# Reordering the passes of a two-matrix feed-forward: three, two, three pairs of F blocks in place of three, three, two

## The chip, the cores and the metric

The kernel runs on one core of a Trainium2 chip. The metric is the device time of one execution in microseconds; three runs of the kernel before gave 1417.96, 1418.64 and 1419.7 us, so the median is 1418.64 us.

## What is computed

Three layers follow each other on 4608 tokens of 512 features:

```python
ret = (scale * q @ k.T) * decay        # retention, 8 batches x 8 heads x 576 positions x 64
x = (ret @ v), rearranged to (4608, 512)
x = mixture of 8 experts, top 1:  gate * (relu(x @ w1[e]) @ w2[e])     # 512 -> 1024 -> 512
h = relu(x @ w_in)                     # 512 -> 2048
out = (h * h) @ w_out                  # 2048 -> 512
```

All inputs are float32 (w_in and w_out are handed over as 64-bit words). The change concerns only the last two lines, the feed-forward with F = 2048.

## The kernel before, in words

`phase0` computes the retention and the routing, `phase12` the experts and meanwhile the preparation of the feed-forward weights, `phase3` (lines 1100 to 1332) the feed-forward. Phase 3 takes the second half of the time, from about 650 us on.

**Tiles.** Phase 3 works on 9 tiles of 512 tokens in the order in which the experts wrote them. Every product is done in a seven-product scheme on 2 x 2 blocks: a tile of x is turned into 7 combinations (`XT`, 7 buffers of 512 KB, one for each combination and none spare), a weight block into 7 combinations, and each operand is split into a high and a low part, so that one product is three matmuls. F is cut in 8 *pairs* of 128-blocks (`NFP = 8`), each pair with its own combined weights for w_in (`WT[0]`) and w_out (`WT[1]`), two 896 KB arrays (high and low) for each.

**Passes.** The weights of all 8 pairs don't fit in SBUF. There are slots for three pairs, so phase 3 goes over the tokens three times. `PASSES` (line 40) says which pairs each pass works on; `T3` (line 1312) lists the steps: pass 0 goes over tiles 0 to 8, pass 1 from 8 down to 0, pass 2 over 0 to 8 again, so that the tile at each turn is the same and its x combinations stay in place. A step has 2 x 7 x (number of pairs) groups of six matmuls of 128x256: `one` (first product, accumulated in PSUM, then squared relu by DVE and ACT into `z`, then split into `h`) and `two` (second product, added by DVE into the output tile `OE`). That is 252 matmuls in a step with three pairs and 168 with two.

**Partial outputs.** There are two output tiles in SBUF, `oe` and `yr` (`OE`, line 1113), used in turn. In passes 0 and 1 a finished tile of partial sums goes to DRAM (`pd`, line 1295, two halves of 512 KB on SP's queue). In passes 1 and 2 `begin(n)` (line 1298) loads the partial sums of tile n back (two halves of 512 KB on SP's queue); a half can be loaded only when the tile that used the buffer before, two steps earlier, has left it. In the last pass (`ends`, line 1260) the finished tile is instead scattered to `out` by four indirect DMAs of 128 rows each, issued by POOL (line 1290); each of them waits for the one before it.

**Loads.** `xprep` (line 1164) computes the x combinations in pass 0 and stores them to `xc`; in passes 1 and 2 it loads the 7 of the next tile (7 x 512 KB). `loadw` (line 1158) loads the weights of a pass into the slots 0, 1 (and 2): those of w_in are planned behind `one` of the last step of the pass before, those of w_out behind its `two`; a slot can be loaded as soon as its last reader is done. All plain DMAs of phase 3 go through SP's queue, which issues them in a fixed order and stands still while the first of them waits.

**Order.** The class `Plan` (line 1033) collects all operations of phase 3 with what they read and write, and orders them by a list scheduler with assumed durations: it looks at the next 400 operations that are left, takes what can start earliest and among these what is due earliest. The order of each engine's program, SP's and POOL's queues included, follows from that. A matrix operation knows nothing of the pass it belongs to, except that pass 0 copies where passes 1 and 2 add, and that the last pass scatters where the others store.

Of the kernel before, what the change touches and what calls it, by code (L numbers as in the profile page):

```python
# [36 lines left out]
CV = 512  # L37
NFP = FF // 256
NCV = 2 * NFP
PASSES = ((0, 1, 2), (3, 4, 5), (6, 7))  # L40
F64MIN = 1.125 * 2.0 ** -15


# [47 lines left out]
def kernel(ctx, tc, qT, kT, kN, vN, modT, w_gate, mbias, w1, w2, w_in, w_out,  # L91
# [929 lines left out]
    def wload2(m, j, pool_, load=True):  # L1021
        for x in range(2):
            held["w", m, j, x] = pool_.tile([P, 7, 256], F32R, tag="w", name=f"w{m}{j}{x}")
            if load:
                sp.dma_start(held["w", m, j, x].bitcast(F32).rearrange("p m c -> p (m c)"), wc[m, PASSES[0][j], x])

# [73 lines left out]
    def phase3():  # L1100
        with ExitStack() as c2:
# [39 lines left out]
            def dma(o, i, kb, r, w, early=False):  # L1141
                plan.add(m_(kb), lambda e: (pool if early else e).dma_start(o, i), r, w, 2.0)
# [15 lines left out]
            def loadw(p, m, j0=0):  # L1158
                for j, fp in list(enumerate(PASSES[p]))[j0:]:
                    for x in range(2):  # L1160
                        dma(WT[m][j][x].bitcast(F32).rearrange("p m c -> p (m c)"), wc[m, fp, x], 917,
                            [], [("w", m, j, x)])
# [40 lines left out]
            def one(n, q, x):  # L1203
                p, t = T3[n]
                if x == 1:
# [12 lines left out]
                         [("w", 0, q, 0), ("w", 0, q, 1), ("x", mx, 0), ("x", mx, 1)], [kp])  # L1218
                last = q == len(PASSES[p]) - 1
                if x == 1:  # L1220
# [37 lines left out]
            def two(n, x):  # L1258
                p, t = T3[n]
                ends = p == len(PASSES) - 1  # L1260
                c = "X" if x in (1, 6, 7, 4) else ("Z" if x == 2 else "Y")
                ps, kr = BR[c], ("R", c)
                for q in range(len(PASSES[p])):
                    u = HS_[n, q]
# [33 lines left out]
            def begin(n):  # L1298
                p, t = T3[n]
                if p and T3[n - 1][1] != t:  # L1300
                    v = VO[n]
                    oe = OE[v]
                    for j0 in (0, 2):
# [3 lines left out]
                            512, [("pd", t, j0)], kk)  # L1307
                if p == len(PASSES) - 1:
                    dma(ixs[n % 2], sd[t * TS:t * TS + TS].rearrange("(j p) -> p j", p=P), 2, [],
# [64 lines left out]
```

## Time and profile before

| what | value |
|---|---|
| median of three runs | 1418.64 us |
| the profiled execution | 1417.05 us, its span 1415.2 us, mean granted clock 0.981 |
| PE busy | 1346.4 us (95%), 10640 matmuls |
| DVE busy | 1024.9 us (72%) |
| ACT busy | 624.1 us (44%) |
| POOL busy | 170.5 us (12%) |
| DMA | 332.43 MB, mean 235 GB/s |

PE's share is that of an engine that sets the pace nearly everywhere, so what matters are the few places where PE stands, and the stretch behind its last matmul. A row of waits says which engine, line and tile waited for what, in total, how often and the longest. A row of the timeline gives start, duration, engine, line, operation, the tile written and those read, how many, and in brackets the idle time of the engine before it and what ended that. SPq is the queue of SyncE, which only issues DMAs.

### The profile page before, as it was taken

The numbers are of one execution on the slowest core, as the hardware profiler recorded it, in microseconds if no ns is written. First come the engines' busy times: TensorE is split into PE (matmuls) and PEld (weight loads), VectorE is DVE, ScalarE is ACT, GpSimd is POOL, SyncE is SP. The second block draws the span as 40 slices with busy tenths as digits, with TensorE's granted clock in tenths as the row PEclk, the third lists the DMA queues.
The fourth block names the chain that finished last, engine by engine and source line by source line (L and its number), as shares of the span: only waits on it lengthen the run. The fifth ranks groups of instructions, "written<-read, shape, count | busy, mean of one in ns | idle before, by whom it ended". The sixth has DMA issues, their size and how long they took to land. (4 is left out here: it accounts for less than half of the span.)

```text
span 1415.2 us, 26973 instructions
## 1 busy us (share of the span) xinstructions
PE 1346.4 (95%) x10640; PEld 1236.5 (87%) x10640; DVE 1024.9 (72%) x2042; ACT 624.1 (44%) x1285; POOL 170.5 (12%) x166
## 2 busy tenths in 40 slices
PE   6999998999999999988999999999999999999985
PEld 5888776888788888878899999999999999999984
DVE  2787766878787788554788877867666777688764
ACT  1444344445445454344555555554334444334321
POOL 3222202100110010000311112000000000011112
PEclk9999999999999999998999999999999999999998
DMA  9988247988999897799544554477445565787672
GB/s 328 382 294 301 91 149 248 258 256 204 326 280 260 237 322 197 232 280 270 202 179 179 199 213 184 191 306 263 165 165 203 214 212 191 275 276 283 224 255 102
DMA packets 143782, 332.43 MB, mean 235 GB/s; under 512 B 20256, under 2 KB 54560, under 8 KB 143648
## 3 DMA queue, kind: packets, MB, share of 16 engines
q1 hardware_dynamic: 135520, 310.06, 65.3%
q0 software_dynamic: 5920, 19.40, 3.6%
q8 instruction: 85, 1.39, 0.4%
q10 hardware_dynamic: 2208, 1.17, 0.3%
q14 instruction: 49, 0.40, 0.1%
HBM read 222.57 MB, written 108.02 MB: 234 GB/s over the span
## 5 line engine op out<-in xcount | busy, mean ns | idle before, releaser
L1153 PE MATMUL bank<-w,h 128*128 128x256 f32 x1008 | 285.0, 283 | 8.9 <-DVE h L1254 8.8
L1151 PE MATMUL bank<-w,h 128*128 128x256 f32 x1008 | 284.1, 282 | 8.2 <-DVE oe L1129 7.3
L1152 PE MATMUL bank<-x,w 128*128 128x256 f32 x1008 | 285.4, 283 | 1.3 <-DVE x L1129 1.3
L1151 PE MATMUL bank<-x,w 128*128 128x256 f32 x1008 | 285.5, 283 | 0.9 <-DMA x<-xc 0.5
L1152 PE MATMUL bank<-w,h 128*128 128x256 f32 x1008 | 283.9, 282 | 1.8 <-DMA w<-wc 1.8
L1153 PE MATMUL bank<-x,w 128*128 128x256 f32 x1008 | 285.0, 283 | 0.0
L1126 ACT ACTIVATE z<-bank 128x256 f32<-128x256 f32 x288 | 109.3, 381 | 275.6 <-PE bank L1153 249.9
L1153 PEld LDWEIGHTS bank<-w,h 128*128 128x128 f32 x1008 | 190.9, 189 | 11.4 <-DVE h L1254 11.2
L1151 PEld LDWEIGHTS bank<-w,h 128*128 128x128 f32 x1008 | 191.2, 190 | 9.8 <-DVE oe L1129 7.9
L1152 PEld LDWEIGHTS bank<-x,w 128*128 128x128 f32 x1008 | 192.9, 191 | 1.9 <-DVE x L1129 1.9
L1151 PEld LDWEIGHTS bank<-x,w 128*128 128x128 f32 x1008 | 192.6, 191 | 1.4 <-ACT z L1126 0.6
L1153 PEld LDWEIGHTS bank<-x,w 128*128 128x128 f32 x1008 | 193.0, 191 | 0.0
L1152 PEld LDWEIGHTS bank<-w,h 128*128 128x128 f32 x1008 | 190.7, 189 | 2.1 <-DMA w<-wc 2.0
L1253 ACT ACTIVATE h<-z 128x512 fp32r<-128x512 f32 (+2 forms) x270 | 158.1, 599 | 68.0 <-DVE z L1129 46.7
L1254 DVE TENSOR_TENSOR h<-z,h 128x512 fp32r<-128x512 f32 (+2 forms) x270 | 172.4, 666 | 3.7 <-ACT h L1253 3.7
L1129 DVE TENSOR_TENSOR z<-z,bank 128x256 f32<-128x256 f32 x216 | 89.5, 417 | 58.9 <-PE bank L1153 53.4
L800 PE MATMUL bank<-hh,wy 128*128 128x512 f32 (+1 forms) x320 | 126.8, 396 | 4.0 <-ACT hh L816 4.0
L800 PE MATMUL bank<-xh,wx 128*128 128x512 f32 (+1 forms) x320 | 124.5, 389 | 3.8 <-PEq L917 3.8
L801 PE MATMUL bank<-xl,wx 128*128 128x512 f32 (+1 forms) x320 | 124.1, 388 | 1.1 <-DVE xl L756 1.1
L801 PE MATMUL bank<-hl,wy 128*128 128x512 f32 (+1 forms) x320 | 124.2, 388 | 0.7 <-DVE hl L817 0.7
L1129 DVE TENSOR_TENSOR z<-z 128x256 f32<-128x256 f32 x288 | 121.8, 451 | 3.1
L802 PE MATMUL bank<-xh,wx 128*128 128x512 f32 (+1 forms) x320 | 124.0, 387 | 0.0
(167 smaller groups left out, 2178.8 us busy)
## 6 DMA issues: line engine op xcount, KB each, us to landing
x<-xc SPq DMA_DIRECT2D x112, 512.0 KB
wr<-w SPq DMA_DIRECT2D x80, 512.0 KB
xc<-x SPq DMA_DIRECT2D x63, 512.0 KB
w<-wc SPq DMA_DIRECT2D x32, 896.0 KB
wc<-cwh SPq DMA_DIRECT2D x16, 896.0 KB
wc<-cwl SPq DMA_DIRECT2D x16, 896.0 KB
pd<-oe SPq DMA_DIRECT2D x24, 512.0 KB
xd<-xs SPq DMA_DIRECT2D x9, 1024.0 KB
```

Source lines behind the costliest of these rows:

```text
L800: pe.matmul(ps, lh, rh, start=first, stop=False)
L801: pe.matmul(ps, lh, rl, start=False, stop=False)
L802: pe.matmul(ps, ll, rh, start=False, stop=last)
L1126: plan.add(a_(c), lambda e: e.activation(o, i, f), r, w)
L1129: plan.add(engs or d_(c), lambda e: e.tensor_tensor(out=o, in0=a, in1=b, op=op), r, w)
L1151: e.matmul(ps[n], lh, rh, start=first and n == 0, stop=False, skip_group_check=True)
L1152: e.matmul(ps[n], lh, rl, start=False, stop=False, skip_group_check=True)
L1153: e.matmul(ps[n], ll, rh, start=False, stop=True, skip_group_check=True)
L1253: plan.add(a_(c), lambda e: e.activation(h[:, 0, a:b], z[:, a + 1:b + 1], AF.Copy), rs, ks[0])
L1254: plan.add(d_(c), lambda e: e.tensor_tensor(out=h[:, 1, a:b], in0=z[:, a + 1:b + 1], in1=h[:, 0, a:b].bitcast(F32), op=ALU.subtract), rs + ...
```

## The change

One line: the middle pass has two pairs and the last has three.

```diff
-PASSES = ((0, 1, 2), (3, 4, 5), (6, 7))
+PASSES = ((0, 1, 2), (3, 4), (5, 6, 7))
```

Everything else follows from `PASSES`: the number of pairs in `one` and `two` of each step, the weights that `loadw` loads at each turn (before: three pairs at the first turn and two at the second; after: two and three), and with them the order that `Plan` makes.

## Rows read from the trace of the kernel before

**Rows 1.** Waits of PE, 942 to 1400 us (passes 1 and 2): total, times, longest.
```profile
PE bank L1151 <- DVE oe L1129: 7.3, 3, 6.2
PE bank L1153 <- DVE h L1254: 1.0, 2, 0.6
PE bank L1151 <- DMA x<-xc: 0.5, 1, 0.5
```

**Rows 2.** Windows: length, busy us (instructions) by engine, clock, DMA share, GB/s.
```profile
core 0: us, PE busy (x) PEld busy (x) DVE busy (x) ACT busy (x) POOL busy (x), PEclk, DMA share, GB/s
971.50:1181.50 210.00, 210.00 (x1773) 210.00 (x1773) 151.92 (x322) 91.40 (x212) 0.00 (x0) 1.00 0.54 194
...
1240.00:1340.00 100.00, 100.00 (x847) 100.00 (x846) 82.15 (x177) 39.19 (x93) 18.07 (x17) 1.00 0.77 267
1340.00:1360.00 20.00, 13.84 (x104) 13.63 (x103) 9.91 (x21) 4.50 (x12) 4.47 (x4) 0.83 0.66 230
1385.00:1400.00 15.00, 12.78 (x95) 11.38 (x93) 12.08 (x26) 3.56 (x8) 4.05 (x4) 1.00 0.35 116
...
1211.00:1231.00 20.00, 19.49 (x162) 19.11 (x162) 14.96 (x32) 8.85 (x20) 0.00 (x0) 1.00 0.89 354
```

**Rows 3.** Timeline of PE and DVE around the one long stand in pass 2.
```profile
1330.63 0.69 DVE L1129 TENSOR_TENSOR yr<-yr,bank 128x512 f32<-128x512 f32 x1 [0.82 <-PE bank L1153]
...
1342.44 0.28 PE L1153 MATMUL bank<-w,h 128*128 128x256 f32 x1
1348.14 0.69 DVE L1129 TENSOR_TENSOR oe<-oe,bank 128x512 f32<-128x512 f32 x1 [6.46 <-DMA oe<-pd]
1348.88 0.58 PE L1151 MATMUL bank<-w,h 128*128 128x256 f32 x1 [6.17 <-DVE oe L1129]
```

**Rows 4.** Timeline of POOL in pass 2: scatters, first of the second to sixth tile.
```profile
1252.58 0.97 POOL L1290 DMA_INDIRECT out<-yr,ix  x1 [3.47 <-DVE z L1129]
...
1340.41 1.05 POOL L1290 DMA_INDIRECT out<-oe,ix  x1 [5.40 <-DMA out<-oe,ix]
1343.96 0.97 POOL L1290 DMA_INDIRECT out<-yr,ix  x1 [2.50 <-issue]
```

**Rows 5.** The tile out: time from a scatter's issue to its landing.
```profile
DMA to landing us min/median/max: 2.7/5.8/7.2
```

**Rows 6.** Timeline of SP's queue: loads of partial sums in pass 2.
```profile
1332.15 0.32 SPq L1142 DMA_DIRECT2D oe<-pd  x1
...
1343.34 0.32 SPq L1142 DMA_DIRECT2D oe<-pd  x1
```

**Rows 7.** Waits of SP's queue, 1200 to 1415 us (pass 2).
```profile
SPq L1142 <- DMA out<-oe,ix: 49.6, 7, 9.8
SPq L1142 <- DMA out<-yr,ix: 35.5, 6, 8.7
```

**Rows 8.** Timeline of POOL, DVE and PE at the end of the kernel.
```profile
1397.58 0.97 POOL L1290 DMA_INDIRECT out<-yr,ix  x1 [2.02 <-DMA out<-yr,ix]
...
1398.44 0.69 DVE L1129 TENSOR_TENSOR oe<-oe,bank 128x512 f32<-128x512 f32 x1 [0.47 <-PE bank L1153]
...
1399.54 0.28 PE L1153 MATMUL bank<-w,h 128*128 128x256 f32 x1
...
1399.86 0.69 DVE L1129 TENSOR_TENSOR oe<-oe,bank 128x512 f32<-128x512 f32 x1 [0.73 <-PE bank L1153]
...
1401.06 0.97 POOL L1290 DMA_INDIRECT out<-oe,ix  x1 [2.51 <-DVE oe L1129]
...
1410.54 0.97 POOL L1290 DMA_INDIRECT out<-oe,ix  x1 [2.02 <-DMA out<-oe,ix]
```

**Rows 9.** Timeline of SP's queue in pass 1: stores, and x loads.
```profile
970.37 2.43 SPq L1142 DMA_DIRECT2D pd<-oe  x2
974.12 1.56 SPq L1142 DMA_DIRECT2D oe<-pd  x2
978.23 7.49 SPq L1142 DMA_DIRECT2D x<-xc  x7
1000.98 2.43 SPq L1142 DMA_DIRECT2D pd<-yr  x2
```

**Rows 10.** Timeline of SP's queue at the second turn: weights of w_out.
```profile
1208.04 3.65 SPq L1142 DMA_DIRECT2D w<-wc  x4
```

## The prediction, made before the changed kernel was run

> **What bounds the kernel now.** First I read the waits of PE, because PE is busy for 95% of the span. In passes 1 and 2 they are three rows [rows 1]: PE stood for 7.3 us because of DVE's adds into `oe`, 6.2 us of it at once, 1.0 us for `h`, and 0.5 us for an x load. No row names weights, so both turns are covered today. Then the windows [rows 2]: in seven steps of pass 1 and in 100 us of pass 2 PE is busy without a gap at full clock, so a step costs what its matmuls cost. A matmul takes 210 / 1773 = 0.118 us there, so a three-pair step of 252 is 29.8 us (a store to the next store is 1000.98 - 970.37 = 30.6 us, [rows 9]) and a two-pair step of 168 is 19.9 us. Only the window from 1340 to 1360 us falls out: 104 matmuls, and a granted clock of 0.83.
>
> The timeline says why. PE's last matmul before the stand starts at 1342.44 us, the next at 1348.88 us, released by a DVE add, and that add by the landing of `oe<-pd` [rows 3]. This half of the partial sums was issued only at 1343.34 us, though the other half was issued at 1332.15 us [rows 6]; what held it is the fourth scatter of the tile that used `oe` before, issued at 1340.41 us [rows 4]. So the chain is scatter, load, add, PE. It is late because scatters are slower than the steps: from 1252.58 to 1343.96 us POOL issued 16 of them, 5.71 us each, 22.8 us for a tile of four [rows 4], against a step of 19.9 us. The queue of scatters falls back by some 2.9 us a step, more when waits add up: the output tile whose add is at 1330.63 us [rows 3] has its first scatter at 1343.96 us, 12.6 us after the add's end. SP's queue stood 85 us in pass 2 for landings of scatters (49.6 + 35.5, [rows 7]). Last I read the end: behind PE's last matmul (1399.82 us) there are 15.4 us of four scatters, each behind the other [rows 8].
>
> **The change part by part.** The matmuls, the DVE and ACT operations and the bytes stay what they are: pairs move from pass 1 to pass 2. What moves is which step has how much time.
>
> *The last pass gets 30 us steps.* Four scatters at 5.71 us are 22.8 us, so each tile's scatters end inside the next step, and no backlog builds up. A buffer is free some 23 us after its tile ends, plus the median landing of 5.8 us [rows 5] and the 4.8 us that the late load took (1343.34 to 1348.14), 34 us. When it is wanted: the tile before in `oe` ended, as an estimate, one step of 19.9 us before the add that ends at 1331.3 us [rows 3], so at 1311.4 us, and PE could go on without the next add into `oe` until 1342.7 us; that is 31 us or 1.57 steps, and 1.57 steps of 29.8 us are 47 us. The cover is 13 us. So the stand goes. Its price is the lost matmuls: 20 us of a full window hold 20 / 0.118 = 169, there were 104, so 65 x 0.118 = 7.7 us; 6.2 us of it is standing, and the rest is the lower clock behind it (granted 0.83 over that window, so a part of it at 1.2 GHz). Bounds: 0, if the stand comes back elsewhere, and 7.7 us. I take 7.7, since nothing near it in time is late next.
>
> The Trainium skill (DMA: Bandwidth & Descriptors, Anatomy of one DMA) gives a software-queue transfer as about 2.0 us plus its bytes at 436 GB/s; for 256 KB that is an estimate of 2.6 us. The trace has 2.7 us as the least and 5.8 us as the median [rows 5], so that figure fits a quiet queue only. By it four scatters would take 4 x (0.97 + 2.6) = 14.3 us, and the last pass would never have fallen behind, as in rival C.
>
> *The end.* In the last tile the first scatter is issued at 1401.06 us, though its adds ended at 1398.44 + 0.69 = 1399.13 us; POOL had issued the tile before only at 1397.58 us and came 2.51 us later, which is backlog again [rows 8]. With three pairs the last product behind that add is three groups of six (18 x 0.118 = 2.1 us) in place of two (1.4 us), so the add ends some 1.3 us before PE does, in place of 0.7. Without backlog the first scatter comes some 0.2 us after the add, 1.1 us before PE's end, where it is 1.24 us behind it now: 2.3 us less. The chain of four behind it (1401.06 to 1415.2, 14.1 us) stays. Bounds: 0, if a scatter is still in the way, and 2.5 us. I take 2.3.
>
> *PE's gaps in the last tile.* From 1385 us to PE's end, 14.8 us, there are 95 matmuls where 14.8 / 0.118 = 125 fit: 30 are missing, 3.5 us, with a few unrecorded ones among them [rows 2]. There is no next tile to work on while the last pair's z and h are made, and DVE is busy 12.08 of 15 us. With three pairs the second product has half as much again to do meanwhile, and the DVE load per matmul is lower (151.92 / 1773 = 86 ns in pass 1 against 82.15 / 847 = 97 ns in pass 2). Bounds: a loss of 0.5 us, if the chain of the last pair is as long and begins later, and a gain of 3.5. I take 1.5.
>
> *The middle pass gets 19.9 us steps.* Each has 7 x loads, two loads and two stores of partial sums, 11 x 0.524 MB = 5.8 MB, 290 GB/s. Pass 2 has the same bytes (the stores are scatters there) and moved 267 GB/s in its even part; right after the second turn it moved 354 GB/s [rows 2], so the demand fits. The buffer of the partial sums, which ruled pass 2, is free at once: from the first store's issue to the load that follows it are 3.75 us [rows 9], against the 23 us of scatters. The x loads stand behind the stores in SP's queue; there they begin 7.9 us after the first store (970.37 to 978.23). I expect this to be hidden, because in pass 2 SP was held up to 9.8 us at once and 85 us in all [rows 7], with the same 19.9 us steps, and x cost PE 0.5 us. Bounds: 0 and 2.9 us a step (rival A). I take 0.5 us in all.
>
> *The turns.* At the first turn four w_out arrays come in place of six; their 3.67 MB at 354 GB/s are 10.4 us, and they are wanted after one `one` of two pairs, 84 x 0.118 = 9.9 us, in part a little later. The second turn of before is this same turn, with its arrays issued at 1208.04 us [rows 10] and no wait of PE for w, but 0.5 us for x [rows 1]. At the second turn of after, slot 2 is free during the whole middle pass, so its four arrays can come early, and the rest has a three-pair step. I expect the 0.5 us for x to change places; bounds 0 and 3 us.
>
> **Sum**, against the profiled execution: -7.7 - 2.3 - 1.5 + 0.5 = -11.0, so 1417.05 - 11.0 = 1406.0 us. The runs' median stands 1.6 us above the profiled execution, which gives 1407.6 us for a median.
>
> **The rivals.**
> *A, slower: SP's queue starves the middle pass of x.* The two stores wait for the step's last adds, and seven x loads stand behind them. If the cover in a 19.9 us step is 5 us and not the 7.9 us from store to x load, each of 8 steps loses 2.9 us, 23 us in all; 1407.6 + 23 = 1430 us. It turns the sign from 11.5 / 8 = 1.4 us a step. For it: there is no spare x buffer, and the demand is 290 GB/s. Against it: the waits of pass 2 just named. By the Trainium skill (DMA: Bandwidth & Descriptors, Queues, rings and completion order) an engine drains one ring in order and shares between queue rows, so stores now stand ahead of x where scatters only shared; no run here shows that apart.
> *B: the weights are late at the turns.* Four arrays arrive in 10.4 us where 9.9 us are there, beside x loads. Two stands of some 3 us and, as after the stand of pass 2, 1.5 us of low clock each (7.7 - 6.2) make 9 us; 1416.5 us. Against it: the turn of before did the same without a wait.
> *C: the stand of pass 2 is no backlog.* Then it comes back in a last pass of any length, and only the end gains: 1407.6 + 7.7 = 1415 us. Against it: POOL's 5.71 us a scatter.
>
> **How the numbers follow.** Forecast 0.73 (own range 1404 to 1412), A 0.08, B 0.12, C 0.07. The forecast's lowest takes all upper bounds of gains, 7.7 + 2.5 + 3.5 = 13.7, so 1418.6 - 13.7 = 1405, and a us below it for run to run; the range goes up into B and C, to 1416. A change under 0.2% (2.8 us) can't be told from none. Faster: the forecast and half of B and of C, 0.82; same: their other halves, 0.1; slower: A, 0.08.
>
> **What would show it.** In the waits of PE no row of some 6 us for `oe`, and no window of passes 1 and 2 under 0.95 of the clock; scatters of a tile that begin within a us or so of its add, with idle POOL between tiles, and SP's waits for `out` far under 85 us; the last tile's first scatter before PE's last matmul. Wrong would be: a row of waits for x or w of over 2 us (A, B), a window of the middle pass with under 160 matmuls in 20 us (A), a stand for `oe` in the last pass (C).

## The result, and the profile after

The changed kernel took 1404.72 us (median of 4 runs, 1404.27 to 1407.67) beside 1418.3 us for the kernel before (4 runs, 1415.94 to 1419.7): 13.6 us less by the medians, a ratio of 0.989 with a 95% interval of 0.9852 to 0.9929. The direction and the mechanism were forecast; the size was forecast too small, 11.0 us. The median lies inside the range, but taken at the ratio, 0.989 x 1418.64 = 1403.0 us lies just under it, and in two further comparisons below the gain was 20 and 17 us by the medians.

PE's waits in passes 1 and 2 after the change (942 to 1400 us; engine, what it waited for, total, times, longest), which answer to [rows 1], and SP's waits for landings of scatters in the whole last pass (1120 to 1403 us), which answer to [rows 7]:

```profile
PE bank L1151 <- DVE oe L1129: 1.5, 1, 1.5
PE bank L1153 <- DVE h L1254: 1.4, 2, 0.7
PE bank L1151 <- ACT h L1253: 0.6, 1, 0.6
...
SPq L1142 <- DMA out<-oe,ix: 22.3, 4, 8.2
SPq L1142 <- DMA out<-yr,ix: 13.2, 3, 8.0
```

The stand of 6.2 us for `oe` is gone; the 1.5 us left is in the last tile. SP's queue stands 35.5 us for scatters in place of 85. Windows of the changed kernel, which answer to [rows 2] (the middle pass, the last pass, the 14.8 us before PE's end, the second turn; columns as there):

```profile
962.00:1100.00 138.00, 138.00 (x1164) 137.89 (x1164) 113.12 (x244) 57.77 (x127) 0.00 (x0) 1.00 0.87 316
...
1160.00:1380.00 220.00, 220.00 (x1855) 219.94 (x1855) 163.19 (x354) 96.12 (x210) 30.56 (x30) 1.00 0.52 183
...
1375.12:1389.92 14.80, 13.34 (x110) 12.90 (x108) 11.18 (x24) 3.40 (x7) 0.97 (x1) 1.00 0.01 2
...
1100.00:1120.00 20.00, 18.75 (x153) 18.22 (x152) 15.66 (x33) 7.32 (x16) 0.00 (x0) 1.00 0.74 289
```

In these windows the short pass moves 316 GB/s and PE doesn't stand once; the last pass is full too, at 183 GB/s. Scatters of the changed kernel, from the timeline of POOL, which answer to [rows 4] and [rows 8]:

```profile
1240.25 0.97 POOL L1290 DMA_INDIRECT out<-yr,ix  x1 [16.87 <-DVE yr L1129]
...
1270.14 0.97 POOL L1290 DMA_INDIRECT out<-oe,ix  x1 [11.99 <-DVE oe L1129]
...
1388.79 0.97 POOL L1290 DMA_INDIRECT out<-oe,ix  x1 [18.06 <-DVE oe L1129]
...
1398.27 0.97 POOL L1290 DMA_INDIRECT out<-oe,ix  x1 [2.02 <-DMA out<-oe,ix]
```

Between two tiles POOL is idle for 10.7 to 18.1 us: no tile's scatters reach the next tile's, and each tile's first scatter starts 0.28 us after the add that it waits for. The time from a scatter's issue to its landing, as [rows 5] has it:

```profile
DMA to landing us min/median/max: 2.7/3.0/4.3
```

This row and [rows 5] can't be set against each other. Each program has 36 scatters, and both profiles recorded the landing of only four of them; the profile of the changed kernel that recorded all 36 has a median of 4.4 us. POOL's timeline has every scatter, and it shows a smaller difference: from the first scatter of a tile to its fourth, over the first seven tiles, 11.3 to 18.7 us in three profiles of the changed kernel and 16.4 to 23.1 us in six of the kernel before. The scatters became somewhat faster; what ended the backlog is that each tile's four now have a step of 29.8 us.

**One measure for all profiles.** Up to the last step of pass 0 the programs of the two orders are the same, and their time there differs from execution to execution. So I take the store at the end of the eighth step of pass 0 as a mark (911.04 us in the first profile of before, 908.99 us after) and split what follows: from the mark to PE's end, and from there to the end of the span.

| profile | mark to PE's end | to the span's end | landing, median us (recorded, of 36) | us a scatter |
|---|---|---|---|---|
| before, first | 488.8 | 15.4 | 5.8 (4) | 5.71 |
| before, second | 490.0 | 14.7 | 4.7 (13) | 5.55 |
| before, third | 500.7 | 14.6 | 5.1 (36) | 6.13 |
| before, fourth | 495.5 | 15.2 | 4.8 (36) | 5.92 |
| before, fifth | 500.4 | 15.3 | 5.4 (36) | 6.26 |
| before, sixth | 500.4 | 14.9 | 4.9 (36) | 6.14 |
| after, three profiles | 480.9, 481.0, 481.7 | 13.0, 13.0, 13.0 | 3.0 (4), 4.1 (8), 4.4 (36) | |
| before, plain stores | 480.5 | 6.3 | 3.0 (4 stores) | |
| after, plain stores | 481.2 | 6.1 | 4.2 (8 stores) | |
| before, no x loads in the last pass | 478.9 | 13.7 | 2.8 (36) | |

The last column is the time from the first scatter of the second tile to the first of the sixth, divided by 16, as in [rows 4].

In the first pair of profiles the change brings 488.8 + 15.4 - 480.9 - 13.0 = 10.3 us behind the mark; the other 2.05 us of the 12.3 us between the spans lie ahead of it. Beside the third, fifth and sixth profile of before it brings over 21 us.

### The profile page after: what moved, and what is told of

The parts are those of the page before. It is cut to its first block, busy times and chain, and to the rows that moved or that the text cites. A ratio compares the mean times of both kernels' runs of the same rounds, so it can differ in the third digit from the quotient of the medians.

```text
span 1402.9 us, 26976 instructions
## 1 busy us (share of the span) xinstructions
PE 1341.8 (96%) x10640; PEld 1233.7 (88%) x10640; DVE 1026.4 (73%) x2051; ACT 626.3 (45%) x1267; POOL 170.9 (12%) x166
## 5 line engine op out<-in xcount | busy, mean ns | idle before, releaser
L1253 ACT ACTIVATE h<-z 128x512 fp32r<-128x512 f32 (+2 forms) x270 | 161.1, 602 | 79.3 <-DVE z L1129 61.4
```

The costliest lines, as they stand in the source:

```text
L1253: plan.add(a_(c), lambda e: e.activation(h[:, 0, a:b], z[:, a + 1:b + 1], AF.Copy), rs, ks[0])
```

## The experiments

Theory: the stand of the last pass and the late end come from scatters that take longer than a two-pair step allows. Rivals: A (SP's queue starves a short middle pass), B (late weights at the turns), C (the stand is no backlog of scatters), and, once the size was off, that the change brings something else besides.

**Both kernels again.** No edit.

> The changed kernel once more, for its ratio and a second profile. Theory (the stand of the last pass and the end are all that changed, and the rest of the 12 us between the two profiled spans is run to run in stages that the change doesn't touch): a ratio of 0.991 to 0.994, 9 to 12 us less, and the time from the store at the end of the eighth step of pass 0 to the end of the span again 493 to 495 us (493.9 in the first profile, 504.2 before). Rival (the change brings more than the stand and the end): a ratio of 0.988 to 0.990, 14 to 17 us less.

> The kernel before once more, for the scatter of unchanged stages and a second profile of the stand. Theory: a ratio of 1.000 within 0.002, again one stand of PE of 4 to 8 us for oe or yr in the last pass, released by a load of partial sums that was held by the fourth scatter of a tile, and the start of phase 3 shifted by up to 4 us against the first profile. Rival (the stand is a mishap of one execution): no stand over 2 us in the last pass.

Measured: the changed kernel 1409.27 us (6 runs, 1407.84 to 1410.39) against 1428.94 us (17 runs, 1418.32 to 1432.98), ratio 0.9873 (0.9842 to 0.9904), 20 us less by the medians and 18 by the ratio; the copy of before 0.9995 (0.9969 to 1.0022). So the size went the rival's way, and even a little beyond it, but the profile went the theory's: from the mark 494.0 us, as 493.9 us the first time. What differs is the kernel before. Its runs spread over 15 us, the changed kernel's over 2.6, and its profiled execution, the second profile of before (1417.24 us), was the shortest of the 12 runs of that copy. It had stands again, but shorter ones, two of up to 3.4 us for `oe` and one of 0.8 for `yr`, so the 4 us expected for one stand were missed. Both kernels once more, with the same picture:

> The changed kernel again, beside its version with the other last step and beside the kernel before. Theory (the stand of the last pass grows with the time of a scatter, which differs from execution to execution, and the changed order hides it): a spread of 5 us or less here against 10 us or more of the kernel before, and 14 to 20 us less. Rival (both spread alike on this chip): the same spread in both.

Measured: 1407.73 us (1405.18 to 1408.77, a spread of 3.6) against 1425.15 us (1412.78 to 1430.54, a spread of 17.8), ratio 0.9889 (0.9849 to 0.9929). As the theory had it.

**Before, profiled four more times.** No edit; the third to the sixth profile of the kernel before.

> The kernel before, one look. Open: over many executions it spreads from 1417 to 1436 us, the changed kernel from 1408 to 1410 us, while both profiled executions of before are at the lower end (1417 us). Theory (stands behind the scatters are longer or more of them in the slower executions): in an execution above 1422 us, more than 8 us of waits of PE for oe or yr in the last pass, and the stages ahead of pass 1 within 4 us of the first profile. Rival (the slower executions lose their time in stages that the change doesn't touch): the last pass as in the first profile, and the start of phase 3 later by as much as the execution is longer.

> As before_look1, another execution, with the same expectations of the theory (the stands grow with the time) and of the rival (the stages ahead of phase 3 do).

> As before_look1, another execution, with the same expectations of the theory (the stands grow with the time) and of the rival (the stages ahead of phase 3 do).

> The kernel before, one more execution beside the one without x loads: time of a scatter in its even part, and PE's stands. Theory: 5.7 to 6.3 us a scatter, stands of 6 to 16 us in all.

Measured: 1430.97, 1426.77, 1431.33 and 1428.33 us. All four show the theory's picture: PE waits 12.0 to 14.6 us for `oe` and `yr` in the last pass. Waits of PE from 942 us on in the fifth profile:

```profile
PE bank L1151 <- DVE oe L1129: 10.9, 3, 6.6
PE bank L1151 <- DVE yr L1129: 2.5, 1, 2.5
```

and three of its stands with what released them, from the timelines of DVE and PE:

```profile
1308.01 0.69 DVE L1129 TENSOR_TENSOR oe<-oe,bank 128x512 f32<-128x512 f32 x1 [3.49 <-DMA oe<-pd]
1308.75 0.43 PE L1151 MATMUL bank<-w,h 128*128 128x256 f32 x1 [3.20 <-DVE oe L1129]
...
1332.22 0.69 DVE L1129 TENSOR_TENSOR yr<-yr,bank 128x512 f32<-128x512 f32 x1 [2.79 <-DMA yr<-pd]
1332.97 0.58 PE L1151 MATMUL bank<-w,h 128*128 128x256 f32 x1 [2.50 <-DVE yr L1129]
...
1360.42 0.69 DVE L1129 TENSOR_TENSOR oe<-oe,bank 128x512 f32<-128x512 f32 x1 [6.85 <-DMA oe<-pd]
1361.17 0.58 PE L1151 MATMUL bank<-w,h 128*128 128x256 f32 x1 [6.55 <-DVE oe L1129]
```

So the stand that the first profile showed once near 1342 us comes here two tiles earlier and then in each of three tiles in a row. Its scatters, first of the second and of the sixth tile, from POOL's timeline:

```profile
1256.15 0.97 POOL L1290 DMA_INDIRECT out<-yr,ix  x1 [2.50 <-DVE z L1137]
...
1356.32 0.97 POOL L1290 DMA_INDIRECT out<-yr,ix  x1 [2.50 <-issue]
```

Sixteen scatters in 100.2 us, 6.26 us each or 25.0 us a tile, against 5.71 us in the first profile [rows 4]. Half a microsecond more a scatter is 2.2 us a tile, so the backlog reaches PE earlier. Over the six profiles the two go together: at 5.55 and 5.71 us a scatter the kernel before has 490.0 and 488.8 us from the mark to PE's end, at 5.92 it has 495.5, and at 6.13 to 6.26 it has 500.4 to 500.7. The third to the fifth profile are from one chip and range from 5.92 to 6.26 us, so it isn't the chip alone; why a scatter takes longer in one execution than in another stays open. From 1300 to 1380 us the fifth profile has 520 matmuls (granted clock 0.89):

```profile
1300.00:1380.00 80.00, 67.74 (x520) 67.13 (x520) 51.03 (x109) 23.18 (x54) 14.60 (x14) 0.89 0.64 228
```

80 us hold 80 / 0.118 = 678; 158 are missing, 18.6 us, where the forecast counted 65 missing ones.

**Plain stores in place of scatters, in both orders.** These kernels leave out the scattering: the rows of `out` stay in the order of the tiles. Shown are the two statements alone, each on one line, without the `plan.add(...)` around them.

```diff
-e.indirect_dma_start(out=out[:, :], out_offset=bass.IndirectOffsetOnAxis(ap=ixs[n % 2][:, j:j + 1], axis=0), in_=oe[:, j, :], in_offset=None)
+e.dma_start(out[t * TS + j * P:t * TS + j * P + P, :], oe[:, j, :])
```

> Passes of three, three, two as before, but each scatter is a plain store of the same 256 KB from POOL's queue to consecutive rows (the rows of out are left in the order of the tiles). Theory (the scatter chain makes the stand): stores don't wait for each other, no stand in the last pass, 7 to 8 us less before PE's end, and 9 to 11 us less behind it (15.4 us become some 5): 16 to 19 us less, about 1400 us. Rival C (the stand is no backlog of scatters): the stand stays, only the end shrinks, 9 to 11 us less, about 1408 us.

> The changed order of passes with the same plain stores in place of scatters. Theory (the order matters only through the scatters): within 3 us of the kernel with plain stores and the old order, about 1400 us. Rival (a short pass at the end costs in itself, by gaps in the last tile or at the turns): 5 us or more below it, about 1394 us. Rival A (a short pass in the middle costs): 3 us or more above it.

Measured beside the 1428.94 us of before: the old order 1401.12 us (1397.57 to 1403.93), ratio 0.9819 (0.9787 to 0.985); the new order 1400.93 us (1397.6 to 1405.17), ratio 0.9818 (0.9785 to 0.9851). Without scatters the two orders take the same time. PE's waits of the old order in passes 1 and 2 are down to this, with no stand for a load of partial sums:

```profile
PE bank L1153 <- DVE h L1254: 1.0, 2, 0.6
PE bank L1151 <- DVE oe L1129: 0.5, 1, 0.5
PE bank L1151 <- ACT h L1253: 0.5, 1, 0.5
PE bank L1153 <- DMA w<-wc: 0.2, 1, 0.2
```

Rival C falls, and so does the idea that a short last pass costs in itself. The gain of the old order was larger than expected, 28 us for 16 to 19, for the reason already told: its mark to PE's end is 480.5 us, so scatters had cost the six profiles of before between 8.3 and 20.2 us there, not 7 to 8.

**A third output tile in the old order.** It lies in the weight slot that a two-pair pass leaves empty, and its sums are rounded to that slot's number format. Not shown are the class that lays the tile there, the rounding, and the wait of a load for that slot.

```diff
-OE = [sb("oe", [P, 4, DM], F32), yr]
+OE = [sb("oe", [P, 4, DM], F32), yr, Halves(*WT[0][2])]
...
-VO.append(VO[-1] if T3[n][1] == T3[n - 1][1] else 1 - VO[-1])
+VO.append(VO[-1] if T3[n][1] == T3[n - 1][1] else (VO[-1] + 1) % (3 if T3[n][0] == 2 else 2))
```

> Passes of three, three, two as before, scatters as before, but the last pass uses a third output tile in turn (in the weight slot that a two-pair pass leaves empty; in this tile the sums are rounded to fp32r). Theory (the stand is the wait for a buffer behind a scatter chain that is slower than a two-pair step): PE's stand of 6 us goes, PE ends 7 to 8 us earlier, but the scatters stay at 5 us or more each and the backlog grows to the end, so the last scatter comes 18 to 24 us after PE's end in place of 10.7: 0 to 5 us less in all. Rival (only the buffer was short, the scatters keep up): 8 us less, with the end 15 us behind PE as before.

Measured: 1423.9 us (12 runs, 1420.43 to 1426.73) against 1424.04 us, ratio 0.9992 (0.9968 to 1.0016): nothing won, within the theory's 0 to 5 us and against the rival's 8. But the way there was only half foreseen. The stand for `oe` went, and PE ended no earlier than in the first profile of before (490.4 us from the mark): of the 9.9 us above the 480.5 of plain stores, 6.8 are now waits for x. The waits of PE, and of SP's queue from 1200 us on:

```profile
PE bank L1162 <- DMA x<-xc: 6.8, 7, 3.7
...
SPq L1153 <- DMA out<-oe,ix: 36.9, 5, 9.3
SPq L1153 <- DMA out<-w,ix: 35.2, 4, 10.4
SPq L1153 <- DMA out<-yr,ix: 26.6, 4, 9.6
```

SP's queue still stood 98.7 us for scatters, and the x loads stand behind those loads of partial sums. The last scatter came 13.0 us behind PE's end, not 18 to 24. A buffer more didn't help where the rate is short; the backlog found the next thing that shares a queue with it.

**No x loads in the last pass, old order.** The last pass works on its first tile's x again, so its sums are not those of the tokens; it has 3.67 MB a step less of DMA.

```diff
-if n == 0 or T3[n - 1][1] == t:
+if n == 0 or T3[n - 1][1] == t or p == 2:
```

> Passes of three, three, two with scatters as before, but the last pass loads no new x combinations (it works on those of its first tile again, 7 x 512 KB a step less of DMA; matmuls, DVE, ACT and scatters as before). Theory (a scatter takes 5 to 6 us there because its bytes share the DMA engines with 267 GB/s of loads): the scatters land in some 3 us, four take about 13 us, no stand, and the end is that of before behind PE: 8 to 20 us less than before. Rival (a scatter is slow because POOL makes its list of addresses beside a DVE that is busy for 82% of the time): landing stays at a median of 4.5 us or more, and the stand stays.

Measured: 1408.25 us (4 runs, 1403.34 to 1408.96) against 1424.08 us (7 runs), ratio 0.9889 (0.9837 to 0.9941), 16 us less. Its landings, and its window in the even part of the last pass:

```profile
DMA to landing us min/median/max: 2.7/2.8/4.7
```
```profile
1240.00:1340.00 100.00, 100.00 (x847) 100.00 (x846) 81.81 (x176) 38.83 (x91) 22.09 (x21) 1.00 0.32 108
```

DVE is as busy as before (81.81 of 100 us, 82.15 in [rows 2]), the DMA load fell from 267 to 108 GB/s, the scatters land in 2.8 us, and PE never waits for `oe` outside the last tile. So the load beside them sets the scatters' time, and not DVE. Whether it does so in the DMA engines or in DRAM is not separated.

**The short pass first: two, three, three.**

```diff
-PASSES = ((0, 1, 2), (3, 4), (5, 6, 7))
+PASSES = ((0, 1), (2, 3, 4), (5, 6, 7))
```
(a second edit, not shown, loads no third slot of weights ahead of the short first pass)

> Passes of two, three, three: the short pass first. Theory (the last pass must be long for the scatters; in pass 0 DVE makes the x combinations as well, and a two-pair step gives it 19.9 us for some 21 to 23 us of work): the end and the last pass as in the changed kernel, but pass 0 loses 1 to 3 us a step against it, 9 to 25 us: 1414 to 1430 us. Rival (any order with three pairs at the end is as good): 1403 to 1407 us.

Measured: 1434.64 us (10 runs) against 1424.04 us, ratio 1.0058 (1.003 to 1.0085): slower than before, and 4.6 us over the theory's upper end. The last pass is without a stand of more than 1.5 us, so that part holds, but a step of pass 0 takes 24.4 us (stores at 686.22 and 856.98 us, seven steps) and not 19.9. Those of the changed kernel aren't free either, 31.8 us for 29.8 (stores at 686.46 and 908.99 us), so a step loses 2.5 us against it, within the expected 1 to 3. What was not expected is the first step: its store comes at 686 us in both kernels, though the short step has 84 matmuls, 9.9 us, less. Window in pass 0:

```profile
700.00:780.00 80.00, 69.33 (x542) 65.50 (x541) 71.48 (x122) 47.88 (x102) 18.53 (x14) 1.00 0.60 225
```

DVE is busy 89% there (71.48 of 80 us); no run tried the step with less work on DVE. Of the three orders the fastest has its short pass where neither the x combinations nor the scatters are made: in the middle.

**Another order of products in the last step**, on top of the change. The sums of 1, 2, 5, 6 and 3 complete the first half of the tile, and its scatters start while products 7 and 4 run.

```diff
-for x in (1, 2, 5, 6, 7, 4, 3):
+for x in (1, 2, 5, 6, 7, 4, 3) if n + 1 < len(T3) else (1, 2, 5, 6, 3, 7, 4):
```
(with the second sum into the quarter that product 7 adds to taken at product 5)

> The changed kernel with the products of the last step in the order 1, 2, 5, 6, 3, 7, 4, so that the first two scatters depend on the sums of 1, 2, 5, 6, 3 and two products (36 matmuls, 4.2 us) are left behind them in place of one (18, 2.1 us). Theory (the chain of four scatters behind the first is the end): the first scatter and the end come 2 us earlier, 1.5 to 2.5 us less than the changed kernel. Rival (the last pair's h is what the new order waits for): PE ends up to 2 us later and nothing is won.

> The changed kernel with the products of the last step in the order 1, 2, 5, 6, 3, 7, 4 again, now on the same chip as the changed kernel itself. Theory (in the first profile the first scatter came 4.3 us before PE's end in place of 1.1, and 14.1 us later all was over as before): 2.5 to 3.5 us less than the changed kernel beside it. Rival (that was one execution): within 1 us of it.

Measured: 1405.65 us against 1424.04 us (ratio 0.9847, 0.9814 to 0.988), and beside the changed kernel 1401.45 us (1400.17 to 1404.99) against 1407.73 us (1405.18 to 1408.77), 6.3 us less by the medians; the ratios to before, 0.9855 and 0.9889, have intervals that overlap. The profiles show 3.4 to 4.2 us of it, more than the first expectation had (1.5 to 2.5): in both, 480.7 us from the mark to PE's end, about what the changed kernel has, and 9.8 us behind it in place of 13.0. The rest lies ahead of the mark (909.48 us here, 912.31 us in the changed kernel beside it), where the programs are the same. The end of the first of them, from the timelines of POOL and PE:

```profile
1394.44 0.97 POOL L1291 DMA_INDIRECT out<-oe,ix  x1 [13.53 <-DVE oe L1129]
...
1398.46 0.28 PE L1153 MATMUL bank<-w,h 128*128 128x256 f32 x1
...
1403.92 0.97 POOL L1291 DMA_INDIRECT out<-oe,ix  x1 [2.02 <-DMA out<-oe,ix]
```

The first scatter is 4.3 us ahead of PE's end; the chain of four is as long as ever. This version beats the kernel before, and in the one direct comparison the changed kernel too, by 3.4 to 4.2 us as far as the profiles show its cause.

## Why the prediction was right in kind and wrong in size

*The step that failed* is the price of the stand: "Bounds: 0, if the stand comes back elsewhere, and 7.7 us. I take 7.7". The mechanism was right (scatter, load, add, PE), but 7.7 us was what one execution lost, and it stood as the upper end as well. Against the plain stores, which leave 480.5 us from the mark to PE's end, six executions of before lost 8.3, 9.5, 20.2, 15.0, 19.9 and 19.9 us. The trace of before held a warning that I read and did not use: the queue of scatters fell back in every step and the buffer's slack was used up in the end, so each longer landing after that point goes into PE's time. Such a term has a long upper side, and one profile gives a sample of it.

That the first pair of profiles comes so near, 10.3 us behind the mark for 11.0, is in part luck: its execution of before is the one from which the price was taken. The further 2.05 us between these two spans lie where the programs are the same. The four runs of before in the result have no profile among them, so how much of their 13.6 us is a longer stand stays open.

*Ahead of it*, 1.6 us were added to get from the profiled execution to the median. The difference between executions lies to a large part in what the change removes: the third, fifth and sixth profile of before have spans 11.2 to 14.2 us longer than the first, and their stretch from the mark to PE's end is 11.6 to 11.9 us longer (by missing matmuls, 8.1 to 10.6 us between 1300 and 1380 us alone). Nothing should have been added for that part; the changed kernel's median lies 0.1 us above its profiled execution.

*The other terms held*, measured in the first pair of profiles. The end: forecast 2.3, measured 15.4 - 13.0 = 2.4 us, with the first scatter 1.1 us before PE's end as worked out. PE's gaps in the last tile: forecast 1.5; 110 matmuls in the last 14.8 us for 95, 15 x 0.118 = 1.8 us. The middle pass: forecast 0.5 us lost, measured none, 1164 matmuls in 138 us. The cover of 13 us for the buffers in the last pass: no add waited for a load there. Its term of 5.8 us for a landing is the median of only four recorded ones; the four profiles with all 36 have 4.8 to 5.4 us.

*The turns* cost more than forecast. I expected an x wait of 0.5 us to change places. There is none, but the window of the second turn holds 153 matmuls for 169, 1.9 us, 1.25 us of it in waits for `h`, where that of before holds 162 [rows 2], and at the first turn PE waits 0.7 us for `h`. The 153 fall under the sign that the prediction set for rival A (under 160 matmuls in 20 us of the middle pass), but the waits are for `h` and not for x. In two of the three profiles no row of these passes names weights, and in the third one does, with 0.3 us: rival B was wrong in its cause and its 9 us, and right that the turns aren't free.

*The rivals.* A fell (its 11.5 us to the turn of the sign should be the sum's 11.0, 1.4 us a step either way): with stores on SP's queue and 316 GB/s no x load was late in the short pass; SP stood 38 us for DVE's adds in all of it. In the third-tile experiment, though, A's mechanism appeared in the place of the stand, with scatters in front of x loads. C fell with the plain stores.

## What to carry to other kernels

When a chain of dependent DMAs is slower than the step that feeds it, its backlog grows step by step, and what it costs at the end moves with every landing time in between (here 8.3 to 20.2 us): price it as a range from the slack to the full shortfall of the remaining steps, and profile several executions before taking one stand as the price. Put such a chain beside the long steps, and the short steps where the transfers are plain. An additional buffer delayed a shortage of rate here, it didn't cure it.

## What the runs showed of the hardware that was not expected

The time of a scatter follows the load beside it: in the last pass of the old order it lands in a median of 4.8 to 5.4 us beside 250 to 261 GB/s (the four profiles with all 36 landings, up to 9.0 us), and in 2.8 us beside 108 GB/s (loads from 1240 to 1340 us). Whether a plain store of the same bytes is hurt as much isn't shown: only four and eight of 36 landings are recorded, with medians of 3.0 us beside 286 GB/s and 4.2 us beside 195.

In the short first pass DVE's additions of 128x256 in SBUF took 678 ns on average (700 to 780 us) against 418 ns in the last pass of the same profile (1200 to 1280 us), and they are long where POOL works beside them: from 690 to 860 us the 32 without a POOL operation beside them took at most 0.43 us, the 24 with one 1.04 us on average. The same is seen on a subtraction in these rows of the timeline:

```profile
742.68 1.43 POOL L1129 TENSOR_TENSOR xt<-yr 128x512 f32<-128x512 f32 x1 [14.84 <-DMA yr<-yd]
...
743.20 1.46 DVE L1254 TENSOR_TENSOR h<-z,h 128x512 fp32r<-128x512 f32 x1
```

A subtraction of that shape takes 0.68 us on average in the later passes; here it takes 1.46 us and ends 0.55 us after POOL's operation. By the Trainium skill (SBUF — State Buffer, Who interferes with whom) the two engines share a pair of ports that is an exclusive lock, and a DVE instruction with two SBUF inputs contends for it with a POOL instruction that reads SBUF. The rows agree roughly: POOL has 0.91 us left when the subtraction starts, and 0.91 + 0.68 is 1.6 us beside the 1.46. So POOL's operations lengthen DVE's work in pass 0. In the first profile of before only 15 of the 84 additions in seven long steps of pass 0 meet one, and the mean is 524 ns. How much of the short step's loss comes from it was not tried.
